# A decode attention kernel whose first weight load is cut into 16 rows and 112 rows

## The chip, the cores and the metric

The kernel runs on one core of a Trainium2 chip. The core has engines that run side by side: TensorE (PE in the profile; its weight loads are PEld), VectorE (DVE), ScalarE (ACT), GpSimd (POOL) and SyncE (SP), which here does nothing but issue loads. Data comes from HBM into the on-chip memory of 128 partitions (SBUF) through 16 DMA engines. Matmul results go to a second on-chip memory, PSUM. The metric is the device time of one execution in microseconds (us). A profile shows one execution, with times counted from the start of its span.

## The reference

Two independent attention blocks, A and B, decode one token each. Both have 32 heads of width 128, a cache of 8192 keys and values per head, and a model width of 512. All inputs are bfloat16. For each block:

```
q      = x @ wq                      # [1,512] @ [512,4096] -> 32 heads x 128
scores = q . k_cache * 128**-0.5     # 32 heads x 8192
p      = softmax(scores)
o      = p @ v_cache                 # 32 heads x 128
y      = o (as 4096) @ wo            # [4096,512] -> [1,512]
```

The output is the two rows y side by side. Each cache is 64 MiB, so there are 256 MiB of keys and values, beside 4 MiB for each of the four weight matrices. Every byte is used once.

## The kernel before

**Tiling.** Heads are taken in quads of four (G = 4), so a block has 8 quads and the whole program 16 (NM = 16, numbered n; n below 8 is block A). In one quad each head has 32 partitions, and each partition holds 256 consecutive keys (T = 256): a quad's K is a tile of 128 partitions x 64 KiB, 8 MiB, and its V the same. `kn` has two such slots for K (NK = 2); `vn` has one for V.

**One quad.** VectorE multiplies K in place by the query, which stands in every partition (L343, four chunks). TensorE adds up the products by matmuls with the identity (L352), VectorE finishes the sum (L363), a maximum over the quad is taken (L369 to L388), ScalarE makes the exponentials (L400), and TensorE multiplies them with V (L421). At the end the heads' outputs are laid out anew and multiplied with wo (L489, L519).

**The queries.** wq has 512 rows of 4096. It is loaded as 128 rows of 32 KiB, partition p getting the rows 4p to 4p+3 of the matrix one after the other. The two wq matrices are laid into `vn`, side by side in each partition, and have to be used up before the first V is loaded there. x is 1 KB for each block, put in partition 0 of the K slot 1. TensorE spreads x over all partitions (L303), ScalarE copies it (L307) into `xb`, TensorE multiplies it with wq (`plan_q`, L321) and ScalarE copies the query to `qbc` (L329).

**What sets the order.** A planner records instructions for each engine with the semaphore counts that they wait for; each engine carries out its own list in order. All loads go out on SyncE's queue, through the helper `dma` (its instruction is L247), in this order: wq of A, x of A, x of B, K of quad 0, wq of B, all of these without a wait; then K of quad 1, which waits until x has been used (`x_ready`), since it overwrites x; then V of quad 0, which waits until wq of B has been used (`q_done[1]`); from there on K of quad n+1, when the slot's old K has been read (`red_done`), and V of quad n, when the V before it has been read (`pv_done`). wo follows at the end, into a K slot. Each DMA adds 16 to its semaphore when it has landed. wq of A and wq of B have a semaphore each (`s_w`), and `dma` returns the semaphore with the count that it will have reached, so that a later wait for the value in `wq_in[a]` covers all transfers recorded on it up to then.

The change touches `load_wq` (L286) and its call for block A (L296). The call for block B (L544) is not touched.

Of the kernel before, what the change touches and what calls it, by code (L numbers as in the profile page):

```python
# [11 lines left out]
P = 128  # L12
# [11 lines left out]
class _Plan:  # L24
# [15 lines left out]
    def op(self, eng, fn, ctr=None, needs=(), inc=1):  # L40

        for m in needs:
            self.wait(eng, m)
        self.prog[eng].append((fn, ctr, inc))
        if ctr is None:
            return None
        ctr.n += inc
        return ctr, ctr.n
# [81 lines left out]
def bass_concat_heads__mha_block_cached__gqa_block_cached__decode_kernel(  # L130
# [16 lines left out]
    wqs = [A_wq, B_wq]  # L147
# [27 lines left out]
    with ExitStack() as st:  # L175
# [8 lines left out]
        def flat(ap):  # L184
            return ap.rearrange("p t d -> p (t d)")
# [3 lines left out]
        wq_buf = [flat(vn[:])[:, a * W:(a + 1) * W] for a in range(NA)]  # L189
# [44 lines left out]
        def ctr(name):  # L234
            return _Ctr(nc, st, name)

        s_x = ctr("s_x")
        s_w = [ctr("s_w%d" % a) for a in range(NA)]
# [7 lines left out]
        def dma(eng, dst, src, c, needs=()):  # L246
            return op(eng, lambda e: e.dma_start(dst, src), c, needs, inc=16)  # L247
# [21 lines left out]
        k_in, v_in, wq_in, wo_in = {}, {}, {}, {}  # L269
# [13 lines left out]
                                [q_done[1] if n == 0 else pv_done[n - 1]]))  # L283
                       for i, (t0, t1) in enumerate(zip(cuts, cuts[1:]))]

        def load_wq(a):  # L286
            wq_in[a] = dma("SP", wq_buf[a], wqs[a].rearrange("(p c) n -> p (c n)", p=P), s_w[a])

        def load_wo(a, g):
            h0, n = WOG[a][g]  # L290
# [2 lines left out]
                              s_wo[a][g], [red_done[NM - 2, NCH - 1]])  # L293


        load_wq(0)  # L296
        x_in = [dma("SP", xrow[0:1, a, :], xs[a][0], s_x) for a in range(NA)][-1]

        for a in range(NA):
# [242 lines left out]

        load_k(0)
        load_wq(1)  # L544
        ahead = len(pl.prog["SP"])
        plan_sel()
# [151 lines left out]
```

## Time and profile before

| what | value |
|---|---|
| median of 3 runs | 666.66 us (666.34 to 666.7) |
| the profiled execution | 666.43 us |
| its span | 665.2 us |
| mean granted TensorE clock | 0.762 |
| busy: PE, DVE, ACT, POOL | 442.8, 340.4, 62.4, 3.0 us |
| read from HBM | 285.21 MB, 429 GB/s over the span |

The profiled execution's own time is 1.2 us more than its span, which runs from the first to the last instruction. In the profile, "busy" for the DMA engines is a share of all 16. In the slices, each digit is a tenth of the slice. A DMA issue is listed under the engine that issues it with a small q (SPq), with the time that the issuing instruction took, not the transfer; the list of DMA issues has the time from issue to landing.

### The profile page before, as it was taken

How to read it: one execution, taken by the hardware profiler on the slowest of the kernel's cores; microseconds unless marked ns; L12 is line 12 of the kernel's file. 1: busy time of each engine (PE TensorE's matmuls, PEld its weight loads, DVE VectorE, ACT ScalarE, POOL GpSimd, SP SyncE). 2: the span in 40 equal slices, each digit the busy share in tenths (PEclk: the TensorE clock that was granted, in tenths of full speed). 3: DMA queues.
4: the chain of work that ended last, by engine and by line, in shares of the span. 5: the costliest groups of instructions: out<-in, count | busy, mean ns of one | idle time of the engine just before them, and what ended most of it. 6: DMA issues, size and time to landing. Idle time of an engine off the chain costs nothing. (4 is left out here: it accounts for less than half of the span.)

```text
span 665.2 us, 12459 instructions
## 1 busy us (share of the span) xinstructions
PE 442.8 (67%) x5649; PEld 254.9 (38%) x5649; DVE 340.4 (51%) x217; ACT 62.4 (9%) x151; POOL 3.0 (0%) x14
## 2 busy tenths in 40 slices
PE   1165876948487594848759484865948386594885
PEld 0022342615235261614426161442626144262655
DVE  1095809366391836639183663908366380825610
ACT  1002002020201002020100202010020202002020
POOL 1000000000000000000000000000000000000000
PEclk9998857769787766978776597877659787765875
DMA  9999999999999999999999999999999999999997
GB/s 378 441 441 438 438 432 422 418 441 434 434 437 441 441 426 414 441 434 434 437 441 437 426 418 441 434 434 437 441 437 426 418 441 434 434 437 441 404 437 315
DMA packets 6076, 285.33 MB, mean 429 GB/s; under 512 B 690, under 2 KB 948, under 8 KB 1204
## 3 DMA queue, kind: packets, MB, share of 16 engines
q1 hardware_dynamic: 6056, 285.22, 99.3%
q8 instruction: 6, 0.10, 0.1%
q14 instruction: 2, 0.02, 0.0%
q10 hardware_dynamic: 12, 0.00, 0.0%
HBM read 285.21 MB, written 0.00 MB: 429 GB/s over the span
## 5 line engine op out<-in xcount | busy, mean ns | idle before, releaser
L352 PE MATMUL rps<-kn,ident 128*128 128x512 bf16 x1024 | 292.9, 454 | 165.9 <-DVE kn L343 165.9
L343 DVE TENSOR_TENSOR kn<-kn,qbc 128x8192 bf16<-128x8192 bf16 x64 | 281.5, 4419 | 96.1 <-DMA kn<-in_A_k_cache_dram 55.9
L352 PEld LDWEIGHTS rps<-kn,ident 128*128 128x128 bf16 x1024 | 112.2, 113 | 333.6 <-issue 258.3
L421 PE MATMUL acc<-pt,vn 128*128 128x4 bf16 x4096 | 109.4, 165 | 9.8 <-issue 4.1
L421 PEld LDWEIGHTS acc<-pt,vn 128*128 128x128 bf16 x4096 | 108.6, 101 | 10.7 <-DMA vn<-in_B_v_cache_dram 4.5
L363 DVE TENSOR_REDUCE s_sb<-rps 128x64 f32<-128x512 f32 x64 | 44.0, 688 | 110.2 <-PE rps L352 110.2
L400 ACT ACTIVATE pt<-s_sb,negb 32x256 bf16<-32x256 f32 x64 | 54.9, 857 | 1.9
L392 ACT ACTIVATE negb<-bmp 128x1 f32<-128x1 f32 x16 | 2.7, 171 | 529.1 <-PE bmp L388 529.1
L430 DVE TENSOR_TENSOR oD<-acc,rinv 128x4 f32 (+1 forms) x16 | 2.6, 162 | 96.2 <-PE acc L421 85.5
L388 PE MATMUL bmp<-gm,hrow 1*128 1x1 f32 x128 | 18.5, 261 | 6.0 <-DVE gm L378 6.0
L388 PEld LDWEIGHTS bmp<-gm,hrow 1*128 1x128 f32 x128 | 17.2, 204 | 10.7 <-DVE gm L378 10.0
L375 PE MATMUL mtp<-ident_f,m 128*1 128x128 f32 x32 | 6.1, 271 | 19.8 <-DVE m L369 19.8
L400 ACT ACTIVATION_READ_ACCUMULATOR pt<-s_sb,negb 32x1 f32 x64 | 15.9, 248 | 0.0
L375 PEld LDWEIGHTS mtp<-ident_f,m 128*1 128x1 f32 x32 | 1.4, 81 | 27.7 <-DVE m L369 27.7
L303 PE MATMUL misc<-ones_bf,kn 1*128 1x128 bf16 x4 | 0.6, 305 | 13.2 <-DMA kn<-in_B_x_dram 13.2
L378 DVE TENSOR_REDUCE gm<-mtp 1x4 f32<-1x128 f32 x16 | 4.4, 278 | 7.5 <-PE mtp L375 7.5
L405 PEld LDWEIGHTS misc<-rsum,ones_f 128*128 128x128 f32 x32 | 6.2, 197 | 3.6 <-issue 1.4
L321 PE MATMUL qyp<-vn,xb 128*32 128x512 bf16 x64 | 6.0, 504 | 2.2 <-ACT qbc L329 1.5
L369 DVE TENSOR_REDUCE m<-s_sb 128x1 f32<-128x256 f32 x16 | 6.7, 420 | 0.5
L489 PE MATMUL qyp<-o,kn 128*128 128x1 bf16 x192 | 5.5, 165 | 1.0 <-issue 0.8
L489 PEld LDWEIGHTS qyp<-o,kn 128*128 128x128 bf16 x192 | 5.4, 102 | 1.3 <-issue 0.8
L329 ACT CAST qbc<-qyp 128x512 bf16<-128x512 f32 x4 | 2.3, 585 | 37.6 <-PE qyp L321 37.6
(41 smaller groups left out, 31.2 us busy)
## 6 DMA issues: line engine op xcount, KB each, us to landing
vn<-in_B_v_cache_dram SPq DMA_DIRECT2D x1, 6144.0 KB, 21.9
vn<-in_A_wq_dram SPq DMA_DIRECT2D x1, 4096.0 KB, 12.2
vn<-in_B_wq_dram SPq DMA_DIRECT2D x1, 4096.0 KB, 39.7
kn<-in_A_wo_dram SPq DMA_DIRECT2D x1, 4096.0 KB, 35.4
kn<-in_B_wo_dram SPq DMA_DIRECT2D x1, 2048.0 KB, 39.9
vn<-in_B_v_cache_dram SPq DMA_DIRECT2D x1, 2048.0 KB, 26.4
kn<-in_B_wo_dram SPq DMA_DIRECT2D x1, 1024.0 KB, 28.4
kn<-in_B_wo_dram SPq DMA_DIRECT2D x1, 512.0 KB, 29.2
```

The lines of the kernel that those rows point to most:

```text
L321: r = e.matmul(qyp[hh * HP:(hh + 1) * HP, :].rearrange("p (i d) -> p i d", d=Dh), xb[:, a, c, hh * HP:(hh + 1) * HP], w, start=(c == 0), s ...
L343: mul_done[n, c] = op("DVE", lambda e: e.tensor_tensor(k, k, qbc[:, nth(n), :].broadcast_to([P, CT, Dh]), ALU.mult), c_mul, [k_in[n], qbc_ ...
L352: r = e.matmul(rps[:, c % 2, :].rearrange("p (t d) -> p t d", d=DW), ident[:], kn[:, i0, c * CT:(c + 1) * CT, i * DW:(i + 1) * DW], start= ...
L363: sr_done[n, c] = op("DVE", lambda e: e.tensor_reduce(s_sb[:, c * CT:(c + 1) * CT], rps[:, c % 2, :].rearrange("p (t d) -> p t d", d=DW), ...
L369: m_done[n] = op("DVE", lambda e: e.tensor_reduce(m1[:], s_sb[:], AX.X, ALU.max), c_dve, [sr_done[n, NCH - 1]])
L375: m = op("PE", lambda e: e.matmul(mtp[0:1, 0:P], m1[:], ident_f[:], start=True, stop=True), c_pe, [m_done[n], i_identf, gm_done.get(n - 1)])
L378: gm_done[n] = op("DVE", lambda e: e.tensor_reduce(gm[:], mtp[0:1, 0:P].rearrange("o (h p) -> o h p", h=G), AX.X, ALU.max), c_dve, [m, nb_ ...
L388: r = e.matmul(bmp[:, 0:1], hrow[0:1, (G - 1 - h) * HP:(G - 1 - h) * HP + P], gm[0:1, h:h + 1], start=(h == 0), stop=(h == G - 1))
L400: p_done[n] = op("ACT", lambda e, h=h, q=q: e.activation(pt[q, :, h], s_sb[q, :], AF.Exp, bias=negb[q, n:n + 1], scale=scale, accum_out=rs ...
L405: m = op("PE", lambda e: e.matmul(misc[:, 0:G], ones_f[:], rsum[:], start=True, stop=True), c_pe, [p_done[n], misc_free[0]])
L421: r = e.matmul(acc[:, 0:G], vn[:, t, :], pt[:, t, :], start=(t == 0), stop=(t == T - 1))
L489: r = e.matmul(qyp[:, i:i + 1], wo_sb[a][:, j, i * P:(i + 1) * P], o2[:, a, j:j + 1], start=(j == 0 and i == 0), stop=(j == HT[a] - 1 and ...
```

## The change

`load_wq` takes a list of row bounds and issues one DMA for each pair of neighbouring bounds. wq of A is loaded by two DMAs: rows 0 to 15 (16 partitions of 32 KiB, 512 KiB), then rows 16 to 127 (112 partitions, 3.5 MiB). wq of B is loaded in one DMA as before. Both pieces of A count on the same semaphore, so that the count in `wq_in[0]` goes from 16 to 32. Bytes, places in the on-chip memory and everything that follows are as before.

```
-        def load_wq(a):
-            wq_in[a] = dma("SP", wq_buf[a], wqs[a].rearrange("(p c) n -> p (c n)", p=P), s_w[a])
+        def load_wq(a, rows=(0, P)):
+            src = wqs[a].rearrange("(p c) n -> p (c n)", p=P)
+            for p0, p1 in zip(rows, rows[1:]):
+                wq_in[a] = dma("SP", wq_buf[a][p0:p1], src[p0:p1], s_w[a])
...
-        load_wq(0)
+        load_wq(0, (0, 16, P))
```

## The prediction

> **What bounds the kernel now.** I read the page's second and third parts first: the span in 40 slices, then the DMA queues.
>
> ```profile
> PE   1165876948487594848759484865948386594885
> DVE  1095809366391836639183663908366380825610
> DMA  9999999999999999999999999999999999999997
> GB/s 378 441 441 438 438 432 422 418 441 434 434 437 441 441 426 414 441 434 434 437 441 437 426 418 441 434 434 437 441 437 426 418 441 434 434 437 441 404 437 315
> q1 hardware_dynamic: 6056, 285.22, 99.3%
> ```
>
> The DMA digit is 9 in every slice but the last, while PE and DVE swing between 0 and 9. SyncE's queue q1 keeps the 16 DMA engines busy for 99.3% of 16 engines' span. No slice moves more than 441 GB/s, whichever tensor it loads. The kernel is one stream of loads, and compute follows it.
>
> Next I cut the span into stretches (columns: stretch, its length, busy time of PE, PEld, DVE, ACT and POOL, granted clock, DMA share, GB/s), to see where the stream is not full.
>
> ```profile
> 0.00:1.50 1.50, 0.00 (x0) 0.00 (x0) 0.01 (x1) 0.71 (x1) 0.88 (x8) 1.00 0.00 0
> 1.50:16.00 14.50, 2.03 (x20) 1.30 (x24) 2.28 (x10) 1.65 (x3) 2.07 (x7) 1.00 1.05 434
> 60.00:640.00 580.00, 402.06 (x4990) 229.70 (x4989) 314.78 (x183) 54.27 (x136) 0.00 (x0) 0.75 1.00 433
> 660.00:665.20 5.20, 2.57 (x76) 1.91 (x73) 0.98 (x5) 0.00 (x0) 0.00 (x0) 0.50 0.34 125
> ```
>
> Two ends are open: 1.50 us before the first byte and part of the last 5.20 us. Between them the share is 1.00 at 433 GB/s, and that rate gives my unit. Sixteen rows of wq, one for each engine, are 16 x 32,768 = 524,288 bytes, which at 433 GB/s take 1.21 us. I call this a set; wq of A is 8 sets, 9.7 us.
>
> Last I asked whether the stream has slack against compute. SyncE's instructions in order of time (start, duration):
>
> ```profile
> 0.80 0.38 SPq L247 DMA_DIRECT2D vn<-in_A_wq_dram  x1
> 1.23 0.32 SPq L247 DMA_DIRECT2D kn<-in_A_x_dram  x1
> 1.61 0.23 SPq L247 DMA_DIRECT2D kn<-in_B_x_dram  x1
> 1.88 0.36 SPq L247 DMA_DIRECT2D kn<-in_A_k_cache_dram  x1
> 2.27 0.53 SPq L247 DMA_DIRECT2D vn<-in_B_wq_dram  x1
> 14.98 0.33 SPq L247 DMA_DIRECT2D kn<-in_A_k_cache_dram  x1
> 54.26 0.33 SPq L247 DMA_DIRECT2D vn<-in_A_v_cache_dram  x1
> 57.76 0.33 SPq L247 DMA_DIRECT2D kn<-in_A_k_cache_dram  x1
> ```
>
> Before the V issue at 54.26 the queue held wq of A, K of quad 0, wq of B and K of quad 1: 4 + 8 + 4 + 8 MiB, 25.2 MB, 58.1 us at 433 GB/s. Started at about 1.8 they last until about 60, so the V issue came some 6 us before the queue ran dry. The DMA share of 1.00 says that it never does run dry. Hence a delay at the head of the stream has no idle DMA time behind it to vanish in, and it moves the end one for one; a gain at the head does the same.
>
> **The change part by part.** The sum is made against the profiled execution: 666.43 us with a span of 665.2; the median of the runs shown, 666.66, lies 0.23 above it.
>
> *The issue.* The first transfer is cut into rows 0 to 15 and rows 16 to 127, so SyncE issues one DMA more, on the same queue and the same semaphore. From its start at 0.80 to the next start at 1.23 an issue costs 0.43 us. The two x loads, K of quad 0 and wq of B are all pushed back by that: 1.23, 1.61, 1.88 and 2.27 become about 1.66, 2.04, 2.31 and 2.70. What hides it is wq's own 9.7 us: K's first byte is not wanted before about 11.5. Without that cover it would cost 0.43 us. The second piece is issued at 1.23 and should have its bytes flowing about 1 us later, while the first set lasts until 2.8 at the earliest. No new wait on an engine is added; the PE waits that name wq_in[0] now ask for a count of 32 instead of 16. I cost this at 0, ends 0 and +0.43.
>
> *The start.* The first 16 us, in 40 slices of 0.4 us (a row's bytes are shown where the row starts):
>
> ```profile
> DMA  0000992109909909909909909909909900009900
> GB/s 0 0 0 0 737 410 82 82 0 655 655 0 492 819 0 492 819 0 492 819 0 492 819 0 492 819 0 410 901 0 819 1807 0 0 0 0 819 1802 0 0
> vn<-in_A_wq_dram SPq DMA_DIRECT2D x1, 4096.0 KB, 12.2
> ```
>
> Rows of the first set start from 1.6 to 3.2, the second set from 3.6; later sets follow every 1.2. So the first set takes about 2.0 us instead of 1.2, and its start lies 0.4 us behind the end of the issue (0.80 + 0.38). If a small first transfer is laid out for all 16 engines sooner, at most 0.8 + 0.4 = 1.2 us is to be gained; nothing excludes that the second piece's engines stumble once more, 0.8 us. Ends -1.2 and +0.8; I take -0.3, between a quarter of the gain and nothing, because most of the first set (737 and 410 GB/s in the first two slices) starts together already and only the stragglers in the 82s can be pulled in.
>
> *Where the rows go.* This is the term that decides. In the profile of before every large transfer fills all 128 partitions at once, and 16 engines write at 433 GB/s, each with 8 partitions' rows. The new first transfer makes 16 engines write into 16 neighbouring partitions, and the second gives each engine 7 rows of the partitions 16 to 127, a different share from the eights that run at full rate now. No row shows what this costs. The lower bound is nothing: every engine keeps its 1/16 of 433 GB/s and the first set takes 1.21 us. For the upper bound, suppose that the 441 GB/s ceiling sits on the way into the on-chip memory: 16 ways, each for 8 of the 128 partitions. In the worst grouping, 8 neighbours per way, 16 neighbouring rows use 2 ways and the first set takes 8 sets' time; every sixteenth partition on a way gives no loss; pairs and fours give 2 and 4.
>
> I then walked the 128 rows step by step on paper, in units of a set: one row for each engine first, then engine e takes rows 16+7e to 22+7e in order, two rows on one way each go at half rate, and K follows in the present even shares. When the slowest engine is done:
>
> - pairs on a way (16 pairs in turn, then again): 6 sets late
> - fours on a way, with the partner block 32 partitions on: 3 sets in the first transfer and 4 in the rest, 7 late
> - fours with the partner block 64 on: 11 late
> - eights on a way: 7 in the first transfer and 1 more, 8 late
>
> The dealing into sevens costs nearly as much as the first transfer, because no run of seven fits groups of two, four or eight: rows 16 and 51, 24 and 59, 88 and 123 meet on one way in the second of these layouts, one pair or two in each of the seven steps. Since a load's semaphore counts all 16 engines, the slowest one sets each landing. So if the ways exist the answer hardly depends on the grouping; I take 7 sets, 7 x 1.21 = +8.5 us, the middle of 6 to 8, and keep 0 and 11 sets (+13.3) as ends.
>
> [...]
>
> *Sum:* 666.43 + 8.5 (rows) - 0.3 (start) + 0 (issue) = 674.6 us, 1.2% slower.
>
> **The rivals.**
>
> *No shared ways: not slower.* The ceiling of 441 GB/s lies in the engines themselves or in the reading of HBM, and the place of a row does not matter. For it: that ceiling is the same for rows of 32 KB (1.50 to 16.00, 434 GB/s) and for the stretch that is nearly all K and V (433), which an engine-bound stream shows too. Against it: nothing, only that the trace has no transfer to fewer partitions to bear it out. It decides if the first set of 16 rows takes under about 2 us. The time is 666.43 - 0.3 = 666.1, from 665.2 (start at its best) to 667.7 (start at its worst and issue uncovered). Being faster by over 0.2%, 1.33 us and about what a measurement of this kernel can tell from no change, would take more than the whole 1.2 us at the start.
>
> *Only the first transfer pays.* The 112 rows are dealt so that each engine keeps to a way of its own, and only 3 sets are lost: 666.43 + 3.6 - 0.3 = 669.8. For it: the 128 rows of today are dealt in some such fitting order, or they would not reach 433 GB/s. Against it: 7 rows do not fill a way of 8, so engines must mix.
>
> *Dealing every sixteenth row.* If engine e takes rows 16+e, 32+e and so on, four neighbours stay together on a way through all 8 steps in the layouts of four: 3 sets lost in each, 24 x 1.21 = 29.1, to 695. Against it: were 128 rows dealt so, the present load would not show sets every 1.2 us in the slices.
>
> **How the numbers follow.** Shared ways with sevens: 0.52, own range 671.5 to 680. Only the first transfer: 0.08. Every sixteenth row: 0.12. No shared ways: 0.28, of which 0.05 lies beyond 0.2% faster and 0.23 within it. So slower 0.72, same 0.23, faster 0.05. The predicted time is that of the likeliest, 674.6. Cases of both signs hold most of the chance, so the range runs from 665.4, which takes in most of the no-sharing case, to 680, 11 sets late; it leaves out the sixteenth-row case and the two thin ends, under 0.2 together.
>
> **What the profile of the changed kernel would show.** The x matmul waits behind the same stream; so does the first K:
>
> ```profile
> 13.23 0.35 PEld L303 LDWEIGHTS misc<-ones_bf,kn 1*128 1x128 bf16 x4 [13.23 <-DMA kn<-in_B_x_dram]
> 32.33 8.76 DVE L343 TENSOR_TENSOR kn<-kn,qbc 128x8192 bf16<-128x8192 bf16 x2 [28.55 <-DMA kn<-in_A_k_cache_dram]
> 663.87 0.27 SPq L247 DMA_DIRECT2D out_dram<-out_q  x1
> ```
>
> If the rows share ways, the slices of 1.6 to 8 us drop to a few times under 433 GB/s; the 16-row load lands 5 to 6 us after its issue instead of about 3; the 112-row load some 20 us after its own; the DVE start at 32.33 moves to 40 to 41; every later issue and the last one at 663.87 by the same 8 us; and the rate from 60 to 640 stays at 433. If there is no sharing, the second set starts at or before 3.6 and 32.33 stays within 1 us. An issue that costs more than its cover shows as a hole in the slices between the two pieces. The prediction is wrong if the early slices keep 433 GB/s, if a later stretch gains DMA idle time, or if the delay at 32.33 does not reach 663.87: then the stream has slack that the DMA share of 1.00 hides.

## The result and the profile after

The changed kernel takes 675.87 us (median of 4, 675.62 to 676.08), the kernel before 666.68 in the same comparison (666.34 to 666.8). That is 9.2 us more, a ratio of 1.014 with a 95% interval of 1.0128 to 1.0153. The profiled execution took 675.93 us with a span of 674.7.

The slices and the queue of the profile after, as on its page:

```profile
DMA  9999999999999999999999999999999999999997
GB/s 214 400 435 432 435 422 432 435 431 427 416 431 435 435 435 436 435 435 435 435 435 435 431 431 435 431 435 435 435 435 435 435 431 431 435 435 435 403 439 302
q1 hardware_dynamic: 6072, 285.22, 99.3%
```

The first slice moves 214 GB/s where it moved 378, and the second 400 where it moved 441. From the third slice to the last but one the rates lie between 403 and 439, where they lay between 404 and 441. The DMA digit is 9 all the same, and the queue is busy for 99.3% as before: a row that takes longer is busy for longer, as the first 16 rows, which took 3.62 us each (median) instead of 2.01. This loss can be read from the GB/s line, not from the busy line. The 16 packets more (6072 instead of 6056) go with the one transfer more: the trace has 692 packets of 4 bytes instead of 676. One of these starts at the end of each of the 16 rows (5.15 to 5.88 us; the rows end from 5.16 to 5.92), and the semaphore of wq of A has 32 updates instead of 16. Those of the 16 rows come from 6.91 to 7.43 us, those of the 112 rows from 21.01 to 22.58; with the last of each the load has landed (6.6 and 21.3 us after its issue).

The span cut at the places where the loss begins and ends (columns as in the prediction; the last is GB/s):

```profile
1.50:5.10 3.60, 0.00 (x0) 0.00 (x0) 2.29 (x10) 0.58 (x1) 2.07 (x7) 1.00 1.00 146
5.10:8.10 3.00, 0.00 (x0) 0.00 (x0) 0.00 (x0) 0.00 (x0) 0.00 (x0) 1.00 0.96 175
8.10:20.20 12.10, 0.00 (x0) 0.00 (x0) 0.00 (x0) 0.00 (x0) 0.00 (x0) 1.00 1.01 260
20.20:60.00 39.80, 16.71 (x88) 6.74 (x88) 17.15 (x6) 2.25 (x4) 0.00 (x0) 1.00 1.04 441
60.00:640.00 580.00, 400.86 (x5005) 228.64 (x5004) 316.41 (x181) 55.27 (x137) 0.00 (x0) 0.75 1.00 432
```

Until 5 to 6 us the 16 rows crawl. From there the 112 rows do, until the first rows of K start behind them at 20.2 to 21.5. From 60 to 640 the stream runs at 432 GB/s, where it ran at 433. Landing times, issues and the instructions that stood in the prediction's last part:

```profile
vn<-in_A_wq_dram SPq DMA_DIRECT2D x1, 3584.0 KB, 21.3
vn<-in_A_wq_dram SPq DMA_DIRECT2D x1, 512.0 KB, 6.6
...
0.80 0.85 SPq L247 DMA_DIRECT2D vn<-in_A_wq_dram  x2
23.44 0.33 SPq L247 DMA_DIRECT2D kn<-in_A_k_cache_dram  x1
63.23 0.33 SPq L247 DMA_DIRECT2D vn<-in_A_v_cache_dram  x1
673.37 0.27 SPq L247 DMA_DIRECT2D out_dram<-out_q  x1
...
41.95 8.76 DVE L345 TENSOR_TENSOR kn<-kn,qbc 128x8192 bf16<-128x8192 bf16 x2 [38.16 <-DMA kn<-in_A_k_cache_dram]
```

VectorE gets its first K at 41.95 instead of 32.33, 9.6 us later. The V issue at 54.26 is now at 63.23 (9.0 later) and the last DMA issue at 673.37 instead of 663.87 (9.5 later). What is lost in the first 21 us is there at the end, within half a microsecond; no later stretch absorbs it.

### The profile page after: what moved, and what is told of

The parts are those of the page before. It is cut to its first block, busy times and chain, and to the rows that moved or that the text cites. A ratio compares the mean times of both kernels' runs of the same rounds, so it can differ in the third digit from the quotient of the medians.

```text
span 674.7 us, 12460 instructions
## 1 busy us (share of the span) xinstructions
PE 441.4 (65%) x5649; PEld 254.4 (38%) x5649; DVE 340.5 (50%) x217; ACT 62.4 (9%) x151; POOL 3.0 (0%) x14
## 3 DMA queue, kind: packets, MB, share of 16 engines
q1 hardware_dynamic: 6072, 285.22, 99.3%
## 6 DMA issues: line engine op xcount, KB each, us to landing
vn<-in_A_wq_dram SPq DMA_DIRECT2D x1, 3584.0 KB, 21.3
```

## The experiments

The theory at the start of the experiments, a supposition that no trace shows as such: rows written into neighbouring partitions share a way into the on-chip memory, with 16 ways in groups of four. "Pairs", "fours" and "eights" are the prediction's layouts, named by how many neighbours share a way; "the walk" is its step-by-step working with the rows, and a set is 16 rows, one for each engine. Two rivals: a price for one transfer more (the piece), and the reading of 16 neighbouring rows from one stretch of HBM (the source). In the table, "more" is the time over the kernel before on the same chip.

| run | us | more | ratio to before, 95% interval |
|---|---|---|---|
| column cut of wq of A | 666.41 | -0.1 | 0.9998 (0.9989 to 1.0008) |
| cut at row 64 | 677.02 | 10.5 | 1.0158 (1.0138 to 1.0179) |
| 512 KiB more, 128 partitions | 667.58 | 1.1 | 1.0016 (1.0006 to 1.0026) |
| 512 KiB more, partitions 0 to 15 | 670.41 | 3.9 | 1.0059 (1.0039 to 1.0079) |
| the same, source rows spread | 670.66 | 4.2 | 1.0064 (1.0041 to 1.0087) |
| 512 KiB more, every eighth partition | 668.67 | 2.2 | 1.0032 (1.0018 to 1.0045) |
| 512 KiB more, partitions 0 to 63 | 669.06 | 2.6 | 1.0039 (1.0023 to 1.0055) |
| 112 rows more | 680.83 | 14.4 | 1.0217 (1.0187 to 1.0247) |
| wq of B cut at row 16 | 676.43 | 10.0 | 1.015 (1.0121 to 1.018) |
| cut at row 112 | 675.62 | 9.2 | 1.0138 (1.0109 to 1.0168) |
| eight transfers of 16 rows | 692.4 | 26.0 | 1.039 (1.036 to 1.042) |
| 16 rows more, seven partitions apart | 671.26 | 4.8 | 1.0072 (1.0049 to 1.0095) |

### Two transfers that fill all partitions

```diff
-            wq_in[a] = dma("SP", wq_buf[a], wqs[a].rearrange("(p c) n -> p (c n)", p=P), s_w[a])
+            src = wqs[a].rearrange("(p c) n -> p (c n)", p=P)
+            for c0, c1 in zip(cols, cols[1:]):
+                wq_in[a] = dma("SP", wq_buf[a][:, c0:c1], src[:, c0:c1], s_w[a])
...
-        load_wq(0)
+        load_wq(0, (0, W // 8, W))
```

> wq of A is loaded by two transfers that both fill all 128 partitions: the first eighth of each row (4 KiB x 128, the same 512 KiB as the 16 rows), then the rest. Theory of the ways (a write into neighbouring partitions shares a way into the memory): no rows meet, so the time is that of the kernel before, 665.5 to 667.5 us. Rival of the piece (a transfer more, its issue and its start cost the time): it stays near the changed kernel, 675 us. Rival of the source (16 neighbouring rows of HBM read from one stretch): 666 to 667 us, as this reads from all rows.

Measured: 666.41 us, no difference from 666.51. Its landings and its first K:

```profile
vn<-in_A_wq_dram SPq DMA_DIRECT2D x1, 3584.0 KB, 11.7
vn<-in_A_wq_dram SPq DMA_DIRECT2D x1, 512.0 KB, 3.6
...
32.34 8.76 DVE L345 TENSOR_TENSOR kn<-kn,qbc 128x8192 bf16<-128x8192 bf16 x2 [28.56 <-DMA kn<-in_A_k_cache_dram]
```

The same 512 KiB land 3.6 us after their issue instead of 6.6, and the first K is as early as in the kernel before (32.33). One DMA more on the queue costs nothing measurable here, so the rival of the piece falls. This small first transfer does not gain anything at the start either.

### The cut at row 64

```diff
-        load_wq(0, (0, 16, P))
+        load_wq(0, (0, P // 2, P))
```

> The changed kernel with the cut at row 64 in place of 16. Theory of the ways, grouping in fours: with the partner block 32 partitions on, each half reaches 8 of 16 ways and wq takes 16 sets instead of 8, +9.7 us, 676 us; with the partner 64 on, nothing is lost, 666.5 us; eights and pairs give +9.7 too. Rival of the piece: like the changed kernel, 675 us, whatever the cut. Rival of the source: each half reads 2 MiB in a stretch, less loss than with 512 KiB, 667 to 671 us.

Measured: 677.02 us, 10.5 more. In the middle of this load the stream keeps the DMA engines busy at half the rate:

```profile
6.70:19.30 12.60, 0.00 (x0) 0.00 (x0) 0.00 (x0) 0.00 (x0) 0.00 (x0) 1.00 1.00 208
```

Of the two layouts of four only the one with the partner block 32 partitions on was expected to lose here (9.7 us); the one with the partner 64 on is out. Pairs and eights are still in.

### 512 KiB more, in four shapes

Each of these five runs is the kernel before, whole, with one load more, issued ahead of wq of A into a part of the K buffer that is not used yet.

```diff
+        room = flat(kn[:, KX])[:, W:2 * W]
+        wsrc = wqs[0].rearrange("(p c) n -> p (c n)", p=P)
+        scr_in = dma("SP", DST, SRC, s_scr)
         load_wq(0)
...
         def load_k(n):
+            if n == KX:
+                wait("SP", scr_in)
```

KX is 1, the K slot and the quad that use this part of the buffer next; its load waits until the load more has landed. W is 16384, the elements of one row of wq as it is loaded (32 KiB).

First the reference, with DST `room[:, 0:W // 8]` and SRC `wsrc[:, 0:W // 8]`:

> The kernel before with one transfer of 512 KiB more ahead of wq of A, into a place of the K buffer that is not used yet: 128 partitions x 4 KiB. This is the reference for the next ones. Ways: the bytes alone, 1.21 us, 667.5 to 668.5 us. Piece: the bytes and the price of a transfer more, up to 676 us. Source: 1.2 us as well.

It takes 1.1 us more, about its bytes. Next 16 neighbouring partitions, `room[0:16]` from `wsrc[0:16]`:

> The same 512 KiB more, as 16 rows of 32 KiB into partitions 0 to 15, from the first 16 rows of wq. Ways: fours +4.8 us (671.5), eights +9.7 (676.4), pairs +2.4 (669.1), every sixteenth partition on a way +1.2 (667.9). Piece: as the transfer into 128 partitions. Source: clearly over 1.2 us, size open.

It takes 3.9 us more, 2.8 more than the reference. The landings, the first row of the reference, the second of the 16 rows:

```profile
kn<-in_A_wq_dram SPq DMA_DIRECT2D x1, 512.0 KB, 3.6
```

```profile
kn<-in_A_wq_dram SPq DMA_DIRECT2D x1, 512.0 KB, 6.6
```

The fours were expected at 4.8 and pairs at 2.4. The 3.9 lies between them and does not decide. The next two cross source and destination: `room[0:16]` from `wsrc[0:P:8]`, and `room[0:P:8]` from `wsrc[0:16]`.

> The 16 rows more into partitions 0 to 15, but read from rows 0, 8, 16 ... 120 of wq, spread over its 4 MiB. Ways: the same time as with neighbouring source rows (fours +4.8 us, 671.5). Source: back to the bytes alone, +1.2 us, 667.9.

> The 16 rows more from the first 16 rows of wq, but put into partitions 0, 8, 16 ... 120. Ways: fours +2.4 us (669.1), eights +1.2 (667.9), pairs +4.8 (671.5), every sixteenth +9.7 (676.4). Source: as with partitions 0 to 15, since the rows read are the same.

With the source rows spread over 4 MiB the loss stays: 4.2 us more, not less than 3.9. With the source rows together and the partitions apart it falls to 2.2. In these runs the place written decides; the rival of the source falls. Fours were expected at 2.4, pairs at 4.8, eights at 1.2: fours are nearest to 2.2. Eights lie at the edge of the interval here, but they had 9.7 for the 16 neighbouring partitions, which cost 3.9. Last, `room[0:64, 0:W // 4]`, 64 rows of 8 KiB:

> 512 KiB more as 64 rows of 8 KiB into partitions 0 to 63. Ways: fours with the partner 32 on, eights or pairs +2.4 us (669.1), fours with the partner 64 on +1.2 (667.9), every sixteenth +4.8 (671.5). Piece: +1.2 or the price seen with 128 partitions. Source: between the two transfers of 16 and 128 rows.

It takes 2.6 us more. The expected 2.4 was that of fours with the partner 32 on, and of pairs and eights as well. So this run speaks against a partner 64 on (1.2) and against dealing every sixteenth row to an engine (4.8), but does not single out the fours.

### The 112 rows alone

The same edit, with `room[16:P]` from `wsrc[16:P]`.

> The kernel before with the second transfer of the change alone more: rows 16 to 127 into partitions 16 to 127, 3.5 MiB, 8.5 us of bytes. Ways, each engine with seven neighbouring rows: fours with the partner 32 on +12.7 us (679.4), with the partner 64 on +18.2 (684.9), eights +9.7 (676.4), pairs +14.5 (681.2). Dealt so that no two engines meet, or no ways: +8.5 (675.2). The first transfer alone being to blame: +8.5.

Measured: 14.4 us more, 5.9 above its bytes. The second piece of the change loses time by itself, twice as much as the first (2.8). The walk through the sevens had 4.2 above the bytes for this load, and pairs 6.0. Pairs would fit here, but not the 3.9 and the 2.2 of the runs before (expected 2.4 and 4.8). With them out, the layout of fours stands and the walk gives too little.

### The pieces in the middle of the stream, and in the other order

```diff
-        load_wq(0, (0, 16, P))
+        load_wq(0)
...
-        load_wq(1)
+        load_wq(1, (0, 16, P))
```

> wq of A in one transfer as before, wq of B in two, cut at row 16: the same two pieces in the middle of the running stream, behind the first K. Ways: +7 sets by the walk, 675.0 us; by the two pieces measured alone (16 rows: 3.90 - 1.07 = 2.8; 112 rows: 14.4 - 8.5 = 5.9) 675.2 us; with the sixteen rows at their full price of 3.6, since no slow start covers a part of it here, 676.0. A loss that belongs to the start of the stream: 666.5 us.

Measured: 676.43 us. So the loss does not need the start of the stream. In the middle it is rather 0.8 us larger (10.0 instead of 9.2). The rows show why: the 16 rows take 4.10 us there (median), where a set takes 1.21; at the start they take 3.62, where the first set of the kernel before takes 2.01 anyway. The next run puts the sixteen rows last:

```diff
-        load_wq(0, (0, 16, P))
+        load_wq(0, (0, P - 16, P))
```

> The changed kernel with the cut at row 112: 112 rows into partitions 0 to 111 first, then 16 rows into 112 to 127. Ways, fours with the partner 32 on: +6.7 us (673.2) by the walk, since engines that are early with their sevens begin the last piece while others are still in theirs; pairs +7.3, eights +9.7. If the two pieces simply add up whatever the order: 675.9.

Measured: 675.62 us, 9.2 more. The walk said 6.7 and is wrong; that the two pieces add up in either order was expected at 675.9.

### Eight transfers of 16 rows

```diff
-        load_wq(0, (0, 16, P))
+        load_wq(0, range(0, P + 1, 16))
```

> wq of A in eight transfers of 16 rows, one row for each engine in each. Ways, fours: four engines share a way through all eight rows, 24 sets, +29 us (695.5); pairs +9.7 (676.2), eights +68 (734). Piece (a fixed price for each transfer more): seven more, well under 1 us each by the column cut, 667 to 668 us.

Measured: 692.4 us, 26.0 more. Pairs (676.2) and eights (734) are far off, fours (695.5) near. The middle of this load:

```profile
9.70:32.60 22.90, 0.00 (x0) 0.00 (x0) 0.00 (x0) 0.00 (x0) 0.00 (x0) 1.00 1.01 114
```

An estimate by the layout of fours, from the three measured rates: four ways carry 114 GB/s here, 28.5 each; the eight of the cut at row 64 carry 208, 26.0 each; all sixteen 433, 27.1 each.

### Seven partitions apart

What remained open was the walk: it let a row without a partner run at full speed, and most rows of the sevens have none.

```diff
         load_wq(0)
+        c0 = NA * D
+        scr_in = dma("SP", flat(kn[:, KX])[0:7 * 15 + 1:7, c0:], quad(ks, 0)[0:16, c0:], s_scr)
...
         def load_k(n):
+            if n == KX:
+                wait("SP", scr_in)
```

> The kernel before with 16 rows more, of 62 KiB each, behind wq of A: into partitions 0, 7, 14 ... 105 of the K buffer that is not used yet, so that the 16 engines start seven partitions apart, as in each step of the walk through the sevens. By the fours with the partner 32 on only two pairs meet (0 with 35, 28 with 63), the other twelve rows have a way of their own. A row alone takes 2.35 us (63,488 bytes at 433/16 GB/s), a row that shares with one other 5.0 (2.56 us for 32 KiB in the cut at row 64). Sharing that slows only those who meet: twelve rows of about 2.35 us and four of about 5, time +5.0 (671.4), as the slowest engine counts. Sharing that slows all 16 engines of the transfer together: sixteen rows of 4 to 5 us, time +4 to +5 as well. No ways: sixteen rows of 2.35, +2.35 (668.8).

Measured: 671.26 us, 4.8 more. The time itself fits both ways of sharing; the rows tell them apart. The stretches show them: the sets of wq run at the full rate up to this load, and then no row starts for 3 us, on any engine.

```profile
5.00:12.00 7.00, 0.00 (x0) 0.00 (x0) 0.00 (x0) 0.00 (x0) 0.00 (x0) 1.00 1.01 435
13.00:16.00 3.00, 0.00 (x0) 0.00 (x0) 0.00 (x0) 0.00 (x0) 0.00 (x0) 1.00 0.00 0
```

Were twelve rows alone on their ways, they would end after 2.35 us, at about 14.5 to 15, and twelve rows of K would start there. The trace's record of each row, 16 rows to a set, says it directly (us):

```
run                           set     shortest  median  longest
before                        2nd       1.21     1.21     1.22
16 rows, seven apart (62 KiB) its one   3.93     4.21     4.47
112 rows alone (32 KiB)       5th       2.09     2.10     2.30
cut at row 64 (32 KiB)        3rd       2.56     2.56     2.57
eight transfers (32 KiB)      3rd       4.57     4.57     4.58
changed kernel, 16 rows       1st       3.31     3.62     3.78
changed kernel, 112 rows      3rd       1.66     1.80     2.28
```

All sixteen rows of the transfer seven apart take 3.9 to 4.5 us. By the layout of fours only four of them share a way. Still none runs at 2.35. The source is not to blame: the rows of K behind it, 64 KiB each from the same tensor, settle at 2.42 us. So, if the layout of fours holds, the meeting of a few slows all 16 engines nearly alike. The set of the changed kernel's 112 rows in the table is one of the fast ones; the medians of the seven are 2.84, 2.26, 1.80, 1.75, 1.98, 2.24 and 2.14.

## Why the prediction was right

The predicted time was 674.6 us, measured were 675.87; the range of 671.5 to 680 for this case holds it. The whole range, 665.4 to 680, says less, since it holds no change as well.

**The stream without slack: right.** The delay at the first K (9.6 us), at the V issue (9.0) and at the last issue (9.5) is one and the same within 0.6 us.

**The issue at nothing: right.** The column cut, with the same two issues, costs -0.1 us. The issues behind it moved by some 0.45 us, as expected (x at 1.70 instead of 1.23).

**The start at -0.3: not confirmed.** The column cut has its first K at 32.34 against 32.33. Its smaller first transfer does not gain at the start; by this run the term should have been 0.

**The rows at 7 sets, 8.5 us: near in the sum, with the layout that fits best of those compared.** No run shows a way itself, or how rows are dealt to the engines. What the runs show is that the partitions written set the loss: 512 KiB from the same 16 rows cost 3.9 us in partitions 0 to 15 and 2.2 in every eighth. In the sum, two sizes were off in opposite directions. The 16 rows were put at 3 sets, 3.6 us, and cost 2.8 over the reference; in the middle of the stream, without the slow start as a cover, the whole change costs 0.8 more. The 112 rows were put at 4 sets, 4.8 us, and cost 5.9 when measured alone. The changed kernel's own rows shift the weight further to the 112. By medians, the 16 rows take 3.62 us instead of 2.01 (1.6 more), the seven sets of the 112 rows 15.0 instead of 8.5 (6.5 more), and the first set of K behind them 3.03 instead of 2.42 (0.6 more). Either way the parts come to 8.7 of the measured 9.2; the remaining 0.5 is not resolved. That the sum came out so near is in part luck: one term was too large, the other too small.

**The step of the walk that failed** is "two rows on one way each go at half rate", with every row that meets no other at the full rate. Where all rows meet by the layout of fours this is close: 2.56 us for two on a way, 4.57 for four, against 1.21 alone. Where only a few meet by that layout, the others were taken to be free, and they are not (3.9 to 4.5 us for every row seven apart, where 2.35 was put for a row alone). Presumably for the same reason the walk gave 6.7 us for the reverse order, which took 9.2. Why the engines slow down together stays open. The rows' records do not say on which engine or partition a row was, so it cannot be excluded that the 112 rows are dealt in another order than the walk's; the transfer seven apart, with its 16 rows all under way at once (a DMA share of 1.06 from 12.10 to 16.08 us), shows the common slowing without that doubt, if the layout is the one that the other runs point to.

**The rivals.** No shared ways (0.28) is excluded by every run into fewer partitions: 512 KiB more cost 2.2 to 4.2 us there, and 1.1 into all 128. Only the first transfer pays, by the 112 rows alone. Every sixteenth row: that would have cost what the eight transfers cost, 26.0 us, and the 112 rows alone lose 5.9. The profile after shows the signs that the prediction named, most of them somewhat larger: the drop in the early slices, 432 GB/s from 60 to 640 (said: 433), the 16-row load landing after 6.6 us (said: 5 to 6), the 112-row load after 21.3 (said: some 20), the first K at 41.95 (said: 40 to 41).

**The layout.** Of the layouts compared here, fours with the partner block 32 partitions on are the one left. The cut at row 64 cost 10.5 us, where a partner 64 on was put at nothing; the eight transfers cost 26.0, where fours were put at 29, pairs at 9.7 and eights at 68. That is how far the times bear it out; a layout that is not among them was not tried.

## What to carry to other kernels

In this kernel a load is better cut along its rows' bytes than along the partitions, so that every piece fills all 128 partitions. Cut in this way (4 and 28 KiB of each row) the second transfer cost nothing measurable (-0.1 us), while the same bytes cut at row 16 cost 9.2 us and at row 64 10.5. For another kernel that is a cut to try first; no run here shows it there. The load stream here never runs dry (a DMA share of 1.00 from 60 to 640 us), and what an early load lost was still lost at the end: the first K was 9.6 us late, and the program took 9.2 us more. The DMA busy share did not show the loss: in the eight transfers it was 1.01 while the rate fell to 114 GB/s, about a quarter of 433. Read the GB/s.

## What the runs showed of the hardware that was not expected

With 16 rows seven partitions apart every one took 3.9 to 4.5 us instead of an estimated 2.35 (63,488 bytes at 433/16 GB/s). If the layout of fours holds, a few rows that meet on a way slow all 16 engines there. By the same layout, and estimated from the measured 208, 114 and 433 GB/s, ways that are shared do not carry exactly what one engine does: 26.0 GB/s with two engines on each, 28.5 with four, 27.1 with one. And an eighth of the load, sent ahead to all partitions, lands after 3.6 us, although the whole 4 MiB in one transfer needs only 12.2: asking for less first did not bring the rest earlier here (the first K at 32.34 against 32.33).
